# GpSimd's small work moved to other steps of attention, the router's last parts joined, and 28 constant matmuls ahead of the first expert's rows

## The chip, the core and the metric

One core of one Trainium2 chip runs the whole program. The metric is the time of one execution on the device in microseconds (us), lower is better. TensorE (PE) has two clock levels, 1.2 and 2.4 GHz; the profile prints the granted share, 0.50 or 1.00, or a mean of both over a stretch. VectorE is DVE, ScalarE is ACT, GpSimd is POOL; SyncE (SP) only issues DMAs, and POOL issues some too.

## What is computed

Clustered attention, then a mixture of 8 experts with one expert for each token, then a gated feed-forward block. Cut to what matters:

```python
# attention: 2 batches, 8 heads, 768 rows, 64 wide, 16 clusters
mask = q_assign[:, :, :, None] == k_assign[:, :, None, :]
scores = where(mask, scale * q @ k.T, -1e9)
attn_out = softmax(scores) @ v                 # 1536 rows of 512
# experts: 1536 rows, 8 experts, 512 -> 1024 -> 512
e_idx = argmax(x @ w_gate); gate_w = softmax(x @ w_gate)[e_idx]
out[rows of e] = gate_w * sigmoid(x @ w_output_gate)[e] * (relu(x @ w1[e]) @ w2[e])
# dense block: 512 -> 2048 -> 512
h = x @ w_in;  result = (h * sigmoid(h)) @ w_out
```

## The kernel before

**Attention.** The 16 heads go in 8 pairs of heads; a pair has 12 steps, so there are 96. A step is 128 query rows of one head. Its scores are made on PE (`qk_mm`, L371 and L373; the cluster mask is a second small product of KB and QB, the tiles that hold the mask rows `mk`), the row minimum on DVE (L392), the exponential on ACT (L394), which gives p in f32. Then p is split into a high and a low f16 part and turned, in one of two ways:

- by DMA: the high part by a copy on ACT (L403) or on DVE (L437, CAST, in steps 4, 5 and 8 of a pair), the low part by a subtraction on POOL (L438), and for two steps together one transposing DMA on SP's queue (L442), called T below;
- on PE, where `onpe` (L376) says so: PE transposes (L418, `turn`), high part on ACT (L424, `high`), low part on DVE (L429, `low2`, two instructions a step).

Seven steps later the product with v follows (`pv`, L462 to L464). A group of steps ends with a division on DVE (L469 to L471) that writes `xb`, the rows of attention's result.

Between the steps stands background work for the pairs that come next. `plan` (L256) gives each part a number r, the step of the pair at which it is issued: loads of q and k, their split (`halves`, ACT L330 and POOL L331, tiles nq and nk), their transposes and the copies of them to QA and KA (L178, L179), the DMAs that copy rows of QA to QB on POOL's queue and of KA to KB on SP's (L298), cluster scores and their one-hot (L193, L203 to L211), masks (L338 to L342), the scale of v (L123 to L142) and the split of v (`split_v`, POOL L152 to L156, for the two heads of a pair). `plan` is called with z true for the first pair. SP also writes zeros into the row buffers of the experts (`xst<-z`, L1195), one write behind most T DMAs. In attention every engine keeps the order in which the program issues; `run` (L476) is the loop over steps that sets this order.

**Router.** When a group of rows of `xb` is done, its part of the router runs as a generator whose pieces are issued one or two to a step: PE transposes (`xtp`, L680), a copy on ACT (L682), logits (`lg`, L689), their sum on DVE (`lacc`, L696), then `route` (L702): one-hot, ranks (`rk`, L731 and L734), gate value and slot on DVE (L723 to L761). Then POOL scatters the rows to the experts' buffers (`scatter`, L772, indirect DMAs, one for 128 rows). `overflow` (L787) counts the rows of each expert (`pn`, L791).

**Experts.** `moe1` (L983) loads and splits eight weight pieces ahead, then `prep(units[0])` reads the first expert's rows back (`xt<-xst`, L782) and turns them on PE (`etp`, L905); `expert` follows with `hp` (L948) and `yp` (L965). After the experts comes the dense block (L1146, L1158). The weights are split into two parts on ACT (L847) and on DVE or POOL (L852).

Of the kernel before, what the change touches and what calls it, by code (L numbers as in the profile page):

```python
# [11 lines left out]
F32 = mybir.dt.float32  # L12
# [18 lines left out]
class Att:  # L31
# [224 lines left out]
    def plan(s, pi, pairs, g0=None, vg=None):  # L256

        nc = s.nc
        u = []
        add = lambda r, f: u.append((r, f))  # L260
        nx = lambda g: lambda: next(g, None)
        if pi + 2 < len(pairs):
            add(3 if g0 else -1, lambda: s.load_qk(*pairs[pi + 2]))
        z = bool(g0)
        b, hp = pairs[pi]
        sp = lambda h, b=b, hp=hp: lambda: s.split_v(b, 2 * hp + h)
        if z:
            for r in (-1, 0, 0, 1, 1):
                add(r, nx(g0))
            for r in (3, 4, 4, 5, 6, 7, 8, 8):  # L270
                add(r, nx(vg))
        for h, r in enumerate((9, 10) if z else (-1, 0)):
            add(r, sp(h))
        if pi == 1:
            s.v1 = s.load_v(1)
        for r in {1: (3, 6, 10), 2: (6, 10), 3: (4, 5, 6, 6)}.get(pi, ()):
            add(r, nx(s.v1))
        if pi + 1 < len(pairs):
            b, hp = pairs[pi + 1]
            if z:  # L280
                for r in range(2):
                    add(r, lambda r=r: s.halves(pairs[1], r))
            hd = [None, None]
            ch = [None, None]
            oh = []

            def start(j):
                hd[j] = s.heads(2 * hp + j, j)
                if j == 0:
                    oh.append(s.ohp.tile([128, NT, 2, 2, C], BF16, tag='oh', name='oh'))  # L290

            def tr(j, a, half):
                if a == 0 and half == 0:
                    start(j)
                s.turned(hd[j][1 + 2 * a], s.nqk[b, hp][a], j, half, (-0.125, 1.0)[a])
                if half:
                    src, dst, e = ((hd[j][1][0:64], hd[j][2][0:64], nc.gpsimd), (hd[j][3][64:128], hd[j][4][0:64], nc.sync))[a]
                    s.defer.append(lambda: e.dma_start(dst.bitcast(F32), src.bitcast(F32)))  # L298

            def sc(j):  # L300
                s.scores(hd[j])
                ch[j] = s.best(s.clb, oh[0], j)
            bst = lambda j: lambda: next(ch[j])
            tr8 = [(j, a, half) for j in range(2) for a in range(2) for half in range(2)]
            for (j, a, half), r in zip(tr8, (2, 2, 3, 3, 4, 4, 5, 5) if z else (-1, -1, -1, 0, 0, 0, 3, 3)):
                add(r, lambda j=j, a=a, half=half: tr(j, a, half))
            for j, (r, r1, r2, r3) in enumerate(((4, 5, 6, 7), (6, 7, 8, 9)) if z else ((1, 2, 3, 4), (4, 5, 6, 7))):
                add(r, lambda j=j: sc(j))
                for q in (r1, r2, r3):
                    add(q, bst(j))  # L310

            def m():
                s.masks(oh[0], hd)
                for j in range(2):
                    s.ready[b, hp, j] = hd[j]
            add(9 if z else 8, m)
        if pi + 2 < len(pairs):
            for i, r in enumerate((5, 6) if not z else (9, 10)):
                add(r, lambda i=i: s.halves(pairs[pi + 2], i))
        u.sort(key=lambda x: x[0])  # L320
        return u
# [54 lines left out]
    def onpe(s, st):  # L376
        g = st['i'] // 2
        n = len(s.steps) // 2

        return (g % 3 == 0 and g >= 6) or g >= n - 6  # L380

    def dve(s, st):

# [65 lines left out]
    def pv(s, st):  # L449
        nc = s.nc  # L450
        b = st['b']
        h = st['hd'][0]
        t = st['t']
        pt = st['pt']
        g = st['g']
        gl = slice(g[0], g[-1] + 1)
        if t == g[0]:
            s.o = s.T('o2')[:, :NT * (D + 2)].rearrange('p (t d) -> p t d', t=NT) if st['j'] and st['pi'] == 7 and (g[-1] == NT - 1) else s.ps_o.tile([128, NT, D + 2], F32, tag='o', name='o')
        o = s.o
        vh, vl = s.vh[b, h]  # L460
        for kt in range(NT):
            nc.tensor.matmul(o[:, t, 0:D + 2], lhsT=pt[:, 0, kt], rhs=vh[:, kt], start=kt == 0, stop=False)  # L462
            nc.tensor.matmul(o[:, t, 0:D], lhsT=pt[:, 0, kt], rhs=vl[:, kt], start=False, stop=False)  # L463
            nc.tensor.matmul(o[:, t, 0:D + 2], lhsT=pt[:, 1, kt], rhs=vh[:, kt], start=False, stop=kt == NT - 1)  # L464
        if t == g[-1]:
            def ev():
                n = len(g)
                rs = s.sm.tile([128, NT], F32, tag='rs', name='rs')[:, :n]
                nc.vector.tensor_scalar(rs, o[:, gl, D], 1e-09, s.inv[b][:, 0, h:h + 1], op0=ALU.add, op1=ALU.mult)  # L469
                nc.vector.reciprocal(rs, rs)  # L470
                nc.vector.tensor_tensor(s.xb[b][:, gl, h * D:(h + 1) * D], o[:, gl, 0:D], rs.unsqueeze(2).to_broadcast([128, n, D]), op=ALU.mult)  # L471
                if h % 2 and s.router:
                    s.late.append((s.now + 1, b, h // 2, g))
            s.oev = ev

    def run(s):  # L476
# [4 lines left out]
        nc = s.nc  # L481
# [19 lines left out]
        traced = nc.cur_bb.bb.instructions  # L501
# [11 lines left out]
        rg = []  # L513
        free = False
        n = len(steps)
# [4 lines left out]
        while done < n:  # L520
# [15 lines left out]
            if 0 <= i < n:  # L536
                s.soft(steps[i])
            s.out()
            if 2 <= i < n + 2 and s.onpe(steps[i - 2]):
                s.low2(steps[i - 2])  # L540
            if 1 <= i < n + 1:
                (s.turn if s.onpe(steps[i - 1]) else s.low)(steps[i - 1])
            now = []
            while todo and todo[0][0] <= i - base:
                now.append(todo.pop(0)[1])
            for f in now[:len(now) // 2]:
                f()
            for k in range(3 if i >= n - 12 else 2):
# [5 lines left out]
                f()  # L554
            if s.late and i >= s.late[0][0]:
                rg.append(s.router(s, *s.late.pop(0)[1:]))
            for k in range(2):
                if rg and (k == 0 or (i - base) % 12 == 9 and i < n - 12) and (free or not (1 <= i < n - 12 and s.onpe(steps[i - 1]))):
                    x = next(rg[0], 0)
                    free = x == 'free'  # L560
                    if x == 0:
                        rg.pop(0)
# [3 lines left out]
        while rg or s.late:  # L566
            if not rg:
                rg.append(s.router(s, *s.late.pop(0)[1:]))
            for _ in rg.pop(0):
                pass  # L570

        prev = {}
        for ins in traced[first:]:
            if ins.engine in prev:
# [21 lines left out]
class Moe:  # L596
# [386 lines left out]
    def moe1(s, w2, free):  # L983
# [19 lines left out]
        def prep(u):  # L1003
            e, h, n = u
            xt = s.rows('xt', s.xo, slice(0, 128), 1) if e == E else s.rows('xt', s.xst, slice(e * CAP + h * 128, e * CAP + (h + n) * 128), n)
            X[u] = (s.labels(xt, n), s.lift(xt, n))
# [1 line left out]
        for i in range(N0):  # L1008
            item(order[0], i)
        s.hold = False  # L1010
        prep(units[0])
        with tc.issue_after(s.lastrow):
            for i in range(N0, 8):
                item(order[0], i)
# [209 lines left out]
```

## Time and profile before

| | |
|---|---|
| time, median of 3 (lowest to highest) | 864.39 us (862.42 to 864.69) |
| the profiled execution: time, span | 858.08 us, 856.0 us |
| mean granted clock of TensorE | 0.925 |
| PE, DVE, ACT, POOL busy in the span | 749.6, 501.9, 415.2, 328.6 us |

The profile is of one execution. Its times are in us from the span's start. A line number is that of the source above; an idle time in brackets stands before an instruction, with what ended it. Attention takes the first 321 us of the span, and the experts and the dense block the rest.

### The profile page before, as it was taken

Reading aid. Unit: us, or ns where it says so; the run is one execution under the profiler, and the core shown is the slowest. Engines: PE = TensorE matmul, PEld = TensorE weight load, DVE = VectorE, ACT = ScalarE, POOL = GpSimd, SP = SyncE. Lnnn points to the kernel's source line nnn. Section 1 sums busy time; section 2 is a strip of 40 time slices with the busy share of each in tenths; the row PEclk is TensorE's granted clock in tenths of the full one; section 3 lists DMA queues with packets and bytes.
Section 4 is the critical chain, followed back from the end, with each engine's and each line's share of the span. In section 5 each row is a group of like instructions: output and inputs, shape, how many; then the busy total and the mean of one; then the engine's idle time right before and its main releaser. Section 6 shows DMA issues by size and latency. Waiting matters only on the chain.

```text
span 856.0 us, 14041 instructions
## 1 busy us (share of the span) xinstructions
PE 749.6 (88%) x5416; PEld 636.4 (74%) x5416; DVE 501.9 (59%) x905; ACT 415.2 (48%) x659; POOL 328.6 (38%) x271
## 2 busy tenths in 40 slices
PE   5859897869799873999899999889899999999994
PEld 4649787868788863888797887567688788878883
DVE  6757688567867777475555687699932322232221
ACT  3756777557485654565444654465522322222221
POOL 1678758385685316644333454335400000000000
PEclk9658999789799985999999999979999999999997
DMA  4399999696676536688664864465400100010001
GB/s 150 65 221 243 205 183 155 134 184 126 136 169 129 121 112 231 217 305 267 210 212 156 295 215 152 172 227 172 148 1 1 49 1 1 0 50 1 1 0 52
DMA packets 135752, 117.09 MB, mean 137 GB/s; under 512 B 100823, under 2 KB 106967, under 8 KB 135680
## 3 DMA queue, kind: packets, MB, share of 16 engines
q1 hardware_dynamic: 131728, 107.06, 48.0%
q0 software_dynamic: 3952, 9.08, 3.7%
q8 instruction: 44, 0.72, 0.4%
q14 instruction: 28, 0.23, 0.1%
HBM read 71.67 MB, written 18.45 MB: 105 GB/s over the span
## 4 chain that ended last, share of the span: by engine, by line
PE 33%; DMA 5%; issue 5%; DVE 4%; POOL 2%; ACT 1%; ACTq 0%; POOLq 0%; DVEq 0%
PE op L1146 13%; PE hp L1158 13%; PE yp L965 3%; DMA x<-ys,f 3%; PE hp L948 2%; POOL w L852 2%; PE hr L930 2%; DMA stage<-in_moe_w_out 1%; DVE stage L1091 1%; DVE stage L1092 1%; DVE stage L1090 1%; DMA stage<-in_moe_w_in 1%; DMA stage<-in_moe_w 1%; DMA out_x<-os 0%; ACT w L847 0%
## 5 line engine op out<-in xcount | busy, mean ns | idle before, releaser
L852 POOL TENSOR_TENSOR w<-stage,w 128x512 fp32r<-128x512 f32 (+1 forms) x54 | 102.2, 1898 | 117.6 <-ACT w L847 115.8
L1158 PE MATMUL hp<-XH,w 128*128 128x512 f32 x384 | 128.5, 406 | 6.8 <-DVE sg L1166 5.6
L847 ACT ACTIVATE w<-stage 128x1024 fp32r<-128x1024 f32 (+1 forms) x104 | 96.4, 940 | 62.4 <-DVE stage L1092 29.9
L438 POOL TENSOR_TENSOR p<-p,p 128x768 f16<-128x768 f32 x60 | 98.4, 1650 | 72.7 <-DVE p L437 42.3
L392 DVE TENSOR_REDUCE m<-sp 128x1 f32<-128x768 f32 x96 | 91.0, 952 | 44.4 <-PE sp L373 35.3
L394 ACT ACTIVATE p<-sp,m 128x768 f32<-128x768 f32 x96 | 86.6, 902 | 54.1 <-DVE m L392 49.3
L1146 PE MATMUL op<-w,GH 128*128 128x512 f32 x384 | 111.7, 397 | 0.0
L1166 DVE TENSOR_TENSOR sg<-hp,sg 128x512 f32<-128x512 f32 x48 | 33.1, 689 | 118.2 <-ACT sg L1165 118.2
L948 PEld LDWEIGHTS hp<-X,w 128*128 128x128 f32 x672 | 86.8, 190 | 11.4 <-DVE HL L951 7.7
L948 PE MATMUL hp<-X,w 128*128 128x256 f32 x672 | 90.0, 284 | 4.6 <-DVE HL L951 4.2
L1158 PEld LDWEIGHTS hp<-XH,w 128*128 128x128 f32 x384 | 73.9, 193 | 26.1 <-DVE sg L1166 7.2
L852 DVE TENSOR_TENSOR w<-stage,w 128x1024 fp32r<-128x1024 f32 x50 | 70.8, 1426 | 28.5 <-ACT w L847 25.1
L462 PE MATMUL o<-vh,pt 128*128 128x66 f16 x576 | 67.7, 202 | 22.2 <-DMA pt<-p 15.9
L1165 ACT ACTIVATE sg<-hp 128x512 f32<-128x512 f32 x48 | 28.6, 597 | 119.5 <-PE hp L1158 118.5
L1146 PEld LDWEIGHTS op<-w,GH 128*128 128x128 f32 x384 | 73.3, 191 | 17.5
L1158 PE MATMUL hp<-XL,w 128*128 128x512 f32 x192 | 77.6, 404 | 2.6 <-DVE XL L852 2.6
L462 PEld LDWEIGHTS <-pt 128*128 128x128 f16 x576 | 55.9, 102 | 29.8 <-DMA pt<-p 17.5
L371 PE MATMUL sp<-KA,QA 128*128 128x384 f32 x192 | 65.8, 426 | 11.8 <-ACT p L394 11.4
L463 PE MATMUL o<-vl,pt 128*128 128x64 f16 x576 | 67.1, 198 | 0.8 <-POOL vl L156 0.8
L1146 PE MATMUL op<-w,GL 128*128 128x512 f32 x192 | 67.0, 399 | 0.6 <-DVE GL L852 0.5
L464 PE MATMUL o<-vh,pt 128*128 128x66 f16 x576 | 66.9, 199 | 0.0
L965 PE MATMUL yp<-w,HH 128*128 128x512 f32 x224 | 63.7, 399 | 0.3 <-ACT HH L950 0.3
(206 smaller groups left out, 1447.2 us busy)
## 6 DMA issues: line engine op xcount, KB each, us to landing
stage<-in_moe_w SPq DMA_DIRECT2D x72, 512.0 KB, 4.7
stage<-in_moe_w_in SPq DMA_DIRECT2D x16, 512.0 KB, 4.7
stage<-in_moe_w_out SPq DMA_DIRECT2D x16, 512.0 KB, 3.5
xst<-z SPq DMA_DIRECT2D x16, 258.0 KB, 3.2
xt<-xst SPq DMA_DIRECT2D x7, 516.0 KB, 4.0
vt<-in_v SPq DMA_DIRECT2D x4, 768.0 KB, 7.2
xt<-x SPq DMA_DIRECT2D x6, 512.0 KB, 5.2
out_x<-os SPq DMA_DIRECT2D x12, 256.0 KB, 2.4
```

Of the source, the lines that this page charges most:

```text
L392: st['min'] = nc.vector.tensor_reduce(m, sv, axis=AX.XY, op=ALU.min).ins
L394: st['exp'] = nc.scalar.activation(p32, sv, AF.Exp, bias=m, scale=-1.0).ins
L438: s.nc.gpsimd.tensor_sub(p16[:, 1], p32, p16[:, 0])
L462: nc.tensor.matmul(o[:, t, 0:D + 2], lhsT=pt[:, 0, kt], rhs=vh[:, kt], start=kt == 0, stop=False)
L463: nc.tensor.matmul(o[:, t, 0:D], lhsT=pt[:, 0, kt], rhs=vl[:, kt], start=False, stop=False)
L464: nc.tensor.matmul(o[:, t, 0:D + 2], lhsT=pt[:, 1, kt], rhs=vh[:, kt], start=False, stop=kt == NT - 1)
L847: s.nc.scalar.activation(hi, src, AF.Copy)
L852: (eng or s.nc.vector).tensor_sub(lo, src, hi)
L948: nc.tensor.matmul(hp, lhsT=W1[k][w][:, f * 128:(f + 1) * 128], rhs=x[:, k, :N], start=n == 0, stop=n == 11)
L965: nc.tensor.matmul(yp, lhsT=h[:, f, i * 128:(i + 1) * 128], rhs=w, start=n == 0, stop=n == 23)
L1146: nc.tensor.matmul(op[i], lhsT=g[:, i * 128:(i + 1) * 128], rhs=w, start=f == 0 and m == 0, stop=f == 15 and m == 2)
L1158: nc.tensor.matmul(hp, lhsT=I[k, f // 8][w][:, fs], rhs=x[:, k], start=n == 0, stop=n == 11)
```

## The change

It has four parts.

1. In `plan`, for the first pair the scale of v, the split of v, the one-hot of the second head and the split of q and k get other step numbers; for the other pairs the split of v moves from steps -1 and 0 to steps 1 and 2, and the split of q and k from steps 5 and 6 to steps 7 and 8.
2. `onpe` also takes the fourth pair of steps of the first pair of heads (steps 6 and 7), so these two are turned on PE, and one T DMA with its two POOL subtractions goes. In `run`, where a step turned on PE is followed by one turned by DMA, its two `low2` instructions stand behind the other step's own instructions, in the background list.
3. In the last two steps a finished group's router part is taken up at once and not a step later, and up to six pieces of it are issued to a step, each behind a `flush` of what was put off.
4. After attention's last PE instruction 28 matmuls of constants (128x128 by 128x512, bf16) are issued, and `prep(units[0])` behind them. Their result is used nowhere.

```diff
             for r in (-1, 0, 0, 1, 1):
                 add(r, nx(g0))
-            for r in (3, 4, 4, 5, 6, 7, 8, 8):
+            for r in (3, 3, 4, 4, 5, 6, 6, 6):
                 add(r, nx(vg))
-        for h, r in enumerate((9, 10) if z else (-1, 0)):
+        for h, r in enumerate((7, 9) if z else (1, 2)):
             add(r, sp(h))
...
-            for j, (r, r1, r2, r3) in enumerate(((4, 5, 6, 7), (6, 7, 8, 9)) if z else ((1, 2, 3, 4), (4, 5, 6, 7))):
+            for j, (r, r1, r2, r3) in enumerate(((4, 5, 6, 7), (7, 8, 8, 9)) if z else ((1, 2, 3, 4), (4, 5, 6, 7))):
...
-            for i, r in enumerate((5, 6) if not z else (9, 10)):
+            for i, r in enumerate((7, 8) if not z else (8, 10)):
                 add(r, lambda i=i: s.halves(pairs[pi + 2], i))
...
-        return (g % 3 == 0 and g >= 6) or g >= n - 6
+        return (g % 3 == 0 and g > 0) or g >= n - 6
...
-                    s.late.append((s.now + 1, b, h // 2, g))
+                    s.late.append((s.now + (s.now < len(s.steps) - 2), b, h // 2, g))
...
-            if 2 <= i < n + 2 and s.onpe(steps[i - 2]):
+            late = 2 <= i < n + 2 and s.onpe(steps[i - 2])
+            if late and (i - 1 >= n or s.onpe(steps[i - 1])):
                 s.low2(steps[i - 2])
+                late = False
...
+            if late:
+                now.append(lambda st=steps[i - 2]: s.low2(st))
...
-            for k in range(2):
-                if rg and (k == 0 or (i - base) % 12 == 9 and i < n - 12) and (free or not (1 <= i < n - 12 and s.onpe(steps[i - 1]))):
+            for k in range(2 if i < n - 2 else 6):
+                if i >= n - 2:
+                    s.flush()
+                if rg and (i >= n - 2 or k == 0 or (i - base) % 12 == 9 and i < n - 12) and (free or not (1 <= i < n - 12 and s.onpe(steps[i - 1]))):
...
+        s.lastpe = [x for x in traced if x.engine == s.nc.tensor.engine][-1]
...
-        prep(units[0])
+
+        idle = s.ps_h.tile([128, 512], F32, tag='h', name='idle')
+        with tc.issue_after(s.att.lastpe):
+            for _ in range(28):
+                r = nc.tensor.matmul(idle, lhsT=s.ones, rhs=s.tri.unsqueeze(1).to_broadcast([128, 4, 128]), start=True, stop=True)
+        with tc.issue_after(r.ins):
+            prep(units[0])
```

**SP in the first pair of heads.** KB<-KA are copies of turned keys, pt<-p is a T DMA, xst<-z a write of zeros, and the four `mk` DMAs bring the mask rows of the second pair of heads. Before:

```order
19 L298 DMA KB<-KA 64x768
20 L442 DMA_TRANSPOSE pt<-p_463 128x24x128
21 L1195 DMA xst<-z 128x516
22 L442 DMA_TRANSPOSE pt<-p_533 128x24x128
23 L1195 DMA xst<-z 128x516
24 L342 DMA QB<-mk 16x768
25 L342 DMA KB<-mk 16x768
```

Now:

```order
19 L298 DMA KB<-KA 64x768
20 L442 DMA_TRANSPOSE pt<-p_464 128x24x128
21 L1208 DMA xst<-z 128x516
22 L342 DMA QB<-mk 16x768
23 L342 DMA KB<-mk 16x768
```

The second T DMA and the write of zeros behind it no longer stand ahead of the `mk` DMAs.

**POOL where the fourth pair of heads begins** (the last steps of the third). L438 is the low part of p (p_1848 before and p_1865 now is the tile of the T DMA that PE waits for in the profile), vh and vl are the split of v, QB<-QA the copies of turned queries. Before:

```order
85 L438 TENSOR_TENSOR p_1848<-p_1846,p_1848 128x768
86 L152 MEMSET vh 128x6x2
87 L154 TENSOR_SCALAR vt_339<-vt_339,vsc_597 128x384
88 L155 CAST vh<-vt_339 128x6x64
89 L156 TENSOR_TENSOR vl<-vt_339,vh 128x384
90 L298 DMA QB<-QA 64x768
91 L438 TENSOR_TENSOR p_1848<-p_1887,p_1848 128x768
92 L152 MEMSET vh 128x6x2
93 L154 TENSOR_SCALAR vt_339<-vt_339,vsc_597 128x384
94 L155 CAST vh<-vt_339 128x6x64
95 L156 TENSOR_TENSOR vl<-vt_339,vh 128x384
96 L298 DMA QB<-QA 64x768
```

Now:

```order
83 L438 TENSOR_TENSOR p_1865<-p_1863,p_1865 128x768
84 L298 DMA QB<-QA 64x768
85 L438 TENSOR_TENSOR p_1865<-p_1904,p_1865 128x768
86 L298 DMA QB<-QA 64x768
87 L152 MEMSET vh 128x6x2
88 L154 TENSOR_SCALAR vt_339<-vt_339,vsc_548 128x384
89 L155 CAST vh<-vt_339 128x6x64
90 L156 TENSOR_TENSOR vl<-vt_339,vh 128x384
```

Both copies of queries and both low parts of the tile now stand ahead of both splits. It is so at the start of every later pair of heads.

**DVE at the end of attention.** L754 to L761 (now L761 to L768) finish the route of the last group but one, L469 to L471 divide the last rows, L696 (now L703) begins the route of the last group. Before:

```order
393 L429 TENSOR_TENSOR pt<-ptp,pt 128x384 x2
394 L696 TENSOR_TENSOR lacc_108<-lacc_108,lg 128x64
...
400 L469 TENSOR_SCALAR rs<-o_4856,vsc_2252 128x2
401 L470 RECIPROCAL rs<-rs 128x2
402 L471 TENSOR_TENSOR xb_67<-o_4856,rs 128x2x64
...
407 L746 TENSOR_REDUCE rank<-r_e_4906 128x4
...
415 L761 RECIPROCAL xb_67<-r_g 128x4
416 L696 TENSOR_TENSOR lacc_108<-lacc_108,lg 128x32
```

Now:

```order
401 L753 TENSOR_REDUCE rank<-r_e_4849 128x4
402 L429 TENSOR_TENSOR pt<-ptp,pt 128x384 x2
...
410 L768 RECIPROCAL xb_67<-r_g 128x4
411 L469 TENSOR_SCALAR rs<-o,vsc_2283 128x2
412 L470 RECIPROCAL rs<-rs 128x2
413 L471 TENSOR_TENSOR xb_67<-o,rs 128x2x64
414 L429 TENSOR_TENSOR pt<-ptp,pt 128x384 x2
415 L469 TENSOR_SCALAR rs<-o_4936,vsc_2283 128x2
416 L470 RECIPROCAL rs<-rs 128x2
417 L471 TENSOR_TENSOR xb_67<-o_4936,rs 128x2x64
418 L703 TENSOR_TENSOR lacc_108<-lacc_108,lg 128x32
```

Before, the last `low2` and the last division (row 402) stood ahead of the end of the first of these routes. Now they stand behind it, and PE likewise makes the last group's three products with v behind that route's ranks.

## Rows read from the trace of the kernel before

**Rows 1.** Stretches: us, length; PE, PEld, DVE, ACT, POOL busy (instructions); granted clock, DMA share, GB/s.

```profile
40.00:50.00 10.00, 4.68 (x23) 3.74 (x23) 9.65 (x25) 4.27 (x5) 6.08 (x4) 0.75 1.07 233
...
130.00:169.00 39.00, 31.95 (x369) 29.39 (x369) 26.41 (x53) 24.02 (x39) 23.11 (x22) 0.82 0.89 155
...
147.40:161.00 13.60, 9.19 (x75) 8.47 (x76) 7.39 (x19) 4.42 (x6) 3.43 (x3) 0.50 1.05 205
...
314.60:333.80 19.20, 3.16 (x49) 2.42 (x45) 14.99 (x62) 6.92 (x11) 9.64 (x10) 0.50 0.35 123
333.80:338.50 4.70, 4.14 (x19) 3.74 (x20) 2.90 (x10) 2.25 (x3) 3.48 (x5) 0.50 1.01 357
```

**Rows 2.** Waits between 20 and 345 us: total, times, longest.

```profile
PE o L462 <- DMA pt<-p: 15.9, 3, 7.3
...
PE sp L373 <- DMA KB<-mk: 5.4, 2, 3.4
```

**Rows 3.** Timeline of PE, the two long waits for T: start, duration.

```profile
151.81 0.24 PE L462 MATMUL o<-vh,pt 128*128 128x66 f16 x1 [6.84 <-DMA pt<-p]
...
190.77 0.24 PE L462 MATMUL o<-vh,pt 128*128 128x66 f16 x1 [7.29 <-DMA pt<-p]
```

**Rows 4.** Timeline of SP's queue ahead of the first of them.

```profile
137.26 0.86 SPq L298 DMA_DIRECT2D KB<-KA  x1
138.23 6.83 SPq L442 DMA_TRANSPOSE pt<-p  x1
```

**Rows 5.** Line L442 over the span: issue in ns, then issue to landing.

```profile
L442 SPq DMA_TRANSPOSE pt<-p x30: 3592/4128/9387, 35.0 to 282.8; - x30
...
DMA to landing us min/median/max: 5.4/6.8/13.7
```

**Rows 6.** Timeline of POOL at the same place.

```profile
134.57 0.58 POOL L298 DMA_DIRECT2D QB<-QA  x1
135.18 1.66 POOL L438 TENSOR_TENSOR p<-p,p 128x768 f16<-128x768 f32 x1
...
139.59 0.58 POOL L298 DMA_DIRECT2D QB<-QA  x1
```

**Rows 7.** Timeline of ACT at the same place.

```profile
133.72 0.87 ACT L179 ACTIVATE QA<-tp 128x384 fp32r<-128x384 f32 x2
```

**Rows 8.** Timeline of SP's queue in the first pair of heads.

```profile
55.29 3.68 SPq L442 DMA_TRANSPOSE pt<-p  x1
59.02 0.57 SPq L1195 DMA_DIRECT2D xst<-z  x1
```

**Rows 9.** DVE's lines L437 and L429: duration in ns, least, median, most.

```profile
L437 DVE CAST p<-p x21: 548/551/2544, 36.9 to 272.7; 128x768 f16<-128x768 f32 x21
...
L429 DVE TENSOR_TENSOR pt<-ptp,pt x72: 544/548/559, 72.8 to 313.0; 128x384 f16<-128x384 f32 x72
```

**Rows 10.** Timeline of DVE, the end of attention.

```profile
315.92 0.29 DVE L471 TENSOR_TENSOR xb<-o,rs 128x128 f32<-128x128 f32 x1
...
318.22 0.18 DVE L761 RECIPROCAL xb<-r_g 128x4 f32<-128x4 f32 x1
...
321.96 0.17 DVE L761 RECIPROCAL xb<-r_g 128x2 f32<-128x2 f32 x1
```

**Rows 11.** Timeline of POOL, the scatters of the last rows.

```profile
318.69 1.09 POOL L772 DMA_INDIRECT xst<-xb,slot  x1 [2.81 <-DVE xb L761]
...
324.47 1.96 POOL L772 DMA_INDIRECT xst<-xb,slot  x1 [0.30 <-DVE w L852]
326.74 0.98 POOL L772 DMA_INDIRECT xst<-xb,slot  x1 [0.30 <-issue]
```

**Rows 12.** Timeline of PE, the first expert.

```profile
333.77 1.97 PE L905 MATMUL etp<-ident,xt 128*128 128x128 f32 x8 [13.01 <-DMA xt<-xst]
...
348.94 0.39 PE L965 MATMUL yp<-w,HL 128*128 128x512 f32 x1
349.17 0.39 PE L965 MATMUL yp<-w,HH 128*128 128x512 f32 x1
```

## The prediction

> **What bounds the kernel now.** I read the stretches first, then PE's waits, then the queues behind the two longest waits, then the end of attention. The change moves nothing behind the first expert's first transposes, so its effect must arise before them: in attention, and in the hand-over to that expert. In attention no engine is full over a pair of heads. The pair from 130 to 169 has PE busy 31.95 of 39.00 us and DMA at 0.89 [rows 1]. PE's waits for DMAs show where the rest goes: three waits for the transposed p, 15.9 us together with the longest 7.3, and two for mask rows, 5.4 us together [rows 2]. The two long ones, 6.84 and 7.29 us, stand at the same place of two consecutive pairs, 39 us apart [rows 3]. In the hand-over PE has nothing to do for 13.01 us, because it waits for the rows read back [rows 12], and the clock granted from 314.6 to 338.5 us is 0.50, the lower of its two levels, so the first 4.70 us of the expert's work are done at half speed [rows 1].
>
> **Part 1, splits of v behind the copies and low parts (POOL), and `low2` behind CAST (DVE).** The first long wait ended at 151.81. Its T was issued at 138.23, 13.6 us before [rows 3, 4], against a median of 6.8 from issue to landing [rows 5]. Its issue itself took 6.83 us, against a median of 4.13 [rows 4, 5]. So this T meets other traffic, and one part of that can be named: a QB<-QA copy issued at 139.59 by POOL [rows 6], after the T. In the new order it stands behind the tile's second low part and ahead of both splits. It needs ACT's copy of the turned queries, which ends at 133.72 + 0.87 = 134.59 [rows 7]. So it can be issued at about 134.6, some 5 us sooner, and be out of the T's way. That is an added wait only for POOL: behind it stand the splits, whose first reader comes steps later. The first copy, 134.57 before, moves ahead of a low part and waits for ACT likewise, about 0.6 us of issue. The T does not start earlier for this: SP's queue is busy up to 138.12 with its own DMAs [rows 4], and only the chain behind the T before it moves, by two `low2` of 0.55 us that no longer stand ahead of the CAST [rows 9], 1.1 us.
>
> What the landing becomes is not in this trace. Bounds: 13.6 (no change, gain 0) and the median 6.8. I take the middle, 10.2, because the pair's loads of q and k and the copy of keys, which stay, are in flight at the same time. Then 3.4 + 1.1 = 4.5 a wait; a part of it is lost, since other waits are then late next (steps follow each other through DVE's minimum), so I take 4.0. Two waits: -8.0, with bounds 0 and -14.1. After the first wait the granted clock is 0.50 for 13.60 us, with PE busy 9.19 in it [rows 1]; a shorter wait may spare a part of this. Half of 9.19 is 4.6 at most for one of them, but PE isn't what sets the pace there; I take -1.0 for both, bounds 0 and -4. The split of q and k, which moves by two steps, and the splits of v in the other pairs lie in POOL's idle time (23.11 busy of 39.00 us [rows 1]): nothing. If that cover is gone, the low part of the next p is late by one split of v, 139.59 - 135.18 - 1.66 = 2.75 us [rows 6], and the T of that p with it.
>
> **Part 2, the first pair of heads.** SP loses a T and a write of zeros, 55.29 to 59.59 us [rows 8], ahead of the mask DMAs of the next pair, so these are issued 4.3 us sooner. PE's two waits for them, 5.4 us [rows 2], would then be over before PE is there. Two steps are turned on PE instead: four more `low2` of 0.55 us, 2.2 us on DVE [rows 9], less nothing, since the high part in these steps was not DVE's. DVE is full there: 9.65 of 10.00 us between 40 and 50 us, where PE has 4.68 and ACT 4.27 [rows 1], so the transposes and copies added to those two are hidden, and DVE's are not. From the other side POOL loses two low parts of 1.66 us [rows 6]. What a DVE instruction can lose beside POOL is seen in CAST: median 0.551, most 2.544 us [rows 9]. Sum: -5.4 + 2.2 = -3.2; since PE will not be at the second wait sooner than DVE lets it, I take -2.0, bounds -5.4 and +2.2.
>
> **Part 3, the router's last parts.** Before, the last division ran at 315.92, the last route but one ended at 318.22 + 0.18 = 318.40, and the last at 321.96 + 0.17 = 322.13 [rows 10]. The first of these routes no longer has the last four `low2` (2.2 us) ahead of it, but part of them were waits of DVE anyway: I take 0.8 us sooner, 317.6. The last group's division now comes behind it: two divisions of some 0.7 us each, two `low2` of 0.55, PE's three products and the transposes between: about 3.2 us, xb at 320.8. From the start of that division to the end of the route were 322.13 - 315.92 = 6.2 us, less 0.3 for the overlap with the other route: 326.7, so +4.6. The scatters bind the two together. Four of the first route went from 318.69 to about 324.2 [rows 11], now from 317.9 to 323.4. The last two, which began at 324.47 and ended at 326.74 + 0.98 = 327.72 [rows 11], 3.25 us, now begin at 326.8 and end at 329.1 (two of 0.98 and a gap of 0.30) to 330.1. From the end of the last scatter to PE's first transposes were 333.77 - 327.72 = 6.05 us [rows 11, 12], unchanged. So the rows come 1.4 to 2.4 us later; I take +2.2, that is 336.0. Bounds: -0.8 (the last route as early as the first) and +4.6.
>
> One of those scatters shows 1.96 us and not 0.98, beside DVE's weight split L852 that it waited on [rows 11]. The Trainium skill (SBUF — State Buffer, SBUF: two separate sides) says that DVE and GpSimd share one port pair as an exclusive lock, and the loser waits for the whole instruction. The trace agrees with its 1.96 and 2.544 beside 0.98 and 0.551. By the rule alone two late scatters that meet DVE's weight splits cost another 1.0, and the tail would be +3.2; the bounds above hold this.
>
> **Part 4, 28 matmuls of 512 columns.** Two such matmuls started 0.23 us apart at the full clock [rows 12], so 28 take 6.5 us at that, 13.1 at half. They start where PE ends its attention work, 333.77 - 13.01 = 320.76 before [rows 12], 1.4 ahead of the last route's end; now 326.7 - 1.4 = 325.3. At half clock from first to last they end at 338.4, 2.4 after the rows (336.0). If the clock rises after as much dense work as between 333.77 and 338.5, 4.7 us [rows 1, 12], then 10 of them take these 4.7 and 18 take 4.2: end at 334.2, before the rows, and the expert starts at the full clock, which gives back half of the 4.73 us, -2.4. I take -1.8, since the clock may be partly lost in the gap of 1.8 us. Bounds: -2.4 and +2.4.
>
> The Trainium skill (TensorE: Matmul & The Clock Gate, What's actually happening) calls the low clock the default, released by activity and lost by idling. This trace's 0.50 from 314.6 to 338.5 agrees. By the rule the matmuls can warm PE, but what ends before the rows can cool again; then the term is 0 and the sum 1.8 worse.
>
> **Sum.** -2.0 - 8.0 - 1.0 + 2.2 - 1.8 = -10.6. On the profiled execution: 858.08 - 10.6 = 847.5. That execution was 6.3 us below the median of the timed runs (864.39). I put the difference on the median: 853.8, so 854.0.
>
> **The rivals.**
>
> *Waits vanish.* If the copies of queries were the cause of the long landings, both T land at the median: the waits lose all of 14.1, the half clock behind them 3: 864.4 - 2.0 - 14.1 - 3 + 0.4 = 845.7, about 845. For it: two waits at one place of the pair, and 13.6 against 6.8. Against it: DMA at 0.89 of 39 us, so the traffic itself must be carried [rows 1].
>
> *DMA sets the pace.* The T is slow because loads of q and k, keys and zeros go at the same time, all of which stay. Then the waits stay: 864.4 - 2.0 + 0.4 = 862.8, give or take 2.5. For it: 0.89 over the pair and 1.05 in the stretch behind the wait [rows 1]. Its issue of 6.83 us began 1.4 us before the copy at 139.59 [rows 4, 6], which speaks against it little.
>
> *Slower: the tail.* Place: between the last division and the first expert's transposes. The last group's route ends 4.6 later and the 28 matmuls run at half clock to their end, 338.4, so the rows wait for PE: 338.4 - 333.8 = +4.6, and there is no clock gained. It decides where attention gives back less than this: with the T waits staying and the first pair at 0 the time is 869.0. For it: PE was at 0.50 with 3.16 busy of 19.20 us [rows 1] just before. Against it: dense work did bring the clock up at 338.5.
>
> **How the numbers follow.** My forecast 0.43 (own range 849 to 859), the waits vanish 0.15, DMA sets the pace 0.22, the tail 0.20. A difference under 0.3%, 2.6 us, can't be told from none here: faster is below 861.8. The first two lie there, 0.58, and of the third 0.08: faster 0.66, same 0.14, slower 0.20. The range: 845 leaves half of the second case below, 0.07, and 868 some 0.12 of the last above.
>
> **What would show it.** Right: the two long waits for T at 4 us or less and T's landing of 9 to 11 there, with QB<-QA issued ahead of it; the wait for mask rows of 3.4 gone; the last L768 at about 326.7, the last scatter's end near 329.5, and a clock of 1.00 in the first `hp`. Wrong: a wait of 6 us or more at the same place, a full DVE that makes the first pair longer, or PE in the 28 matmuls when the rows are there.

## The result and the profile after

The changed kernel took 856.07 us (median of 20 runs, 848.32 lowest) against 865.44 us for the kernel before, measured beside it. The ratio is 0.9862, 95% interval 0.9835 to 0.9889, which on 864.4 us is 11.9 us less, with 9.6 to 14.3 as the interval. The ratio leaves out the runs that lie over 1.5% above the fastest of their kernel (five of the 20, one of them 1068.87 us at a mean granted clock of 0.646, and one of the 20 of the kernel before); the medians of all runs differ by 9.4 us.

The profiled execution of the changed kernel took 859.21 us, span 857.1, no less than that of before (858.08). So a sum over the two spans explains nothing here. Each stage has to be read for itself, and the last part of this section says what went wrong in that execution.

**The two long waits.** The waits of PE in the changed kernel, in the same stretch and columns as [rows 2]:

```profile
PE o L462 <- DMA pt<-p: 4.1, 3, 1.7
...
PE sp L373 <- DMA QB<-mk: 2.1, 1, 2.1
...
PE sp L373 <- DMA KB<-mk: 0.7, 1, 0.7
```

The timeline of PE at the two places of [rows 3]:

```profile
143.91 0.23 PE L462 MATMUL o<-vh,pt 128*128 128x66 f16 x1 [1.74 <-DMA pt<-p]
...
177.18 0.24 PE L462 MATMUL o<-vh,pt 128*128 128x66 f16 x1 [1.53 <-DMA pt<-p]
```

The 6.84 and 7.29 us have become 1.74 and 1.53. The timeline of POOL ahead of the first of them, which answers to [rows 6]:

```profile
129.29 0.58 POOL L298 DMA_DIRECT2D QB<-QA  x1 [0.94 <-ACT QA L179]
129.90 1.67 POOL L438 TENSOR_TENSOR p<-p,p 128x768 f16<-128x768 f32 x1
131.71 0.53 POOL L298 DMA_DIRECT2D QB<-QA  x1
```

And SP's queue, which answers to [rows 4]:

```profile
133.06 0.51 SPq L298 DMA_DIRECT2D KB<-KA  x1
133.68 8.09 SPq L442 DMA_TRANSPOSE pt<-p  x1
```

The second copy of queries is issued 2.0 us before the T now, where it was 1.4 us behind it. The first waits 0.94 us for ACT, with nothing urgent behind. The issue of this T took 8.09 us all the same, more than the 6.83 of before. From minimum to minimum, the fourth pair takes 33.6 us where it took 38.8, and the fourth and fifth together 66.5 where they took 77.7. The first pair takes 36.2 us where it took 39.7; but its first minimum stood 2.7 us later in this execution (26.65 against 23.96), so its end came only 0.8 us sooner. Stretches of the changed kernel (columns as in [rows 1]), the first and fourth pair of heads:

```profile
26.60:62.80 36.20, 27.61 (x162) 23.32 (x161) 27.24 (x48) 25.60 (x37) 26.29 (x22) 0.86 0.63 137
...
127.10:160.70 33.60, 31.67 (x366) 29.19 (x364) 26.89 (x53) 23.68 (x39) 23.24 (x21) 0.85 0.92 179
```

**The end of attention.** The timeline of DVE, which answers to [rows 10]:

```profile
302.72 0.18 DVE L768 RECIPROCAL xb<-r_g 128x4 f32<-128x4 f32 x1
...
306.83 0.22 DVE L469 TENSOR_SCALAR rs<-o,vsc 128x2 f32<-128x2 f32 x1 [2.03 <-remote]
...
307.29 0.29 DVE L471 TENSOR_TENSOR xb<-o,rs 128x128 f32<-128x128 f32 x1
...
313.33 0.17 DVE L768 RECIPROCAL xb<-r_g 128x2 f32<-128x2 f32 x1
```

The timeline of POOL's last scatters, which answers to [rows 11]:

```profile
313.77 1.77 POOL L779 DMA_INDIRECT xst<-xb,slot  x1 [5.64 <-DVE o_cnt L801]
315.85 0.98 POOL L779 DMA_INDIRECT xst<-xb,slot  x1 [0.30 <-issue]
```

Four scatters of the first route are done early, at 308.14, and then POOL waits 5.64 us for the last route. The last minimum of attention in the timeline of DVE, in the profile of before and then here:

```profile
305.91 0.96 DVE L392 TENSOR_REDUCE m<-sp 128x1 f32<-128x768 f32 x1 [0.55 <-PE sp L373]
...
291.86 0.96 DVE L392 TENSOR_REDUCE m<-sp 128x1 f32<-128x768 f32 x1 [0.55 <-PE sp L373]
```

Measured from it, the last division came 10.0 us later before and 15.4 now, and PE's first transposes 27.9 us before and 30.8 now. Of the 15.4, 2.03 us are a stop of DVE, marked "remote" above: the trace has no releaser for it on this core.

**The clock.** Stretches of the changed kernel from the constant matmuls on:

```profile
312.00:317.10 5.10, 5.10 (x19) 1.79 (x16) 3.55 (x12) 4.93 (x7) 3.02 (x3) 0.50 0.13 46
317.10:323.90 6.80, 4.69 (x25) 2.30 (x23) 6.38 (x18) 0.55 (x2) 0.61 (x3) 1.00 0.66 229
323.90:330.70 6.80, 6.21 (x27) 5.85 (x28) 5.72 (x16) 3.53 (x6) 5.28 (x5) 0.50 0.97 341
```

And PE's timeline there:

```profile
317.29 3.40 PE L1022 MATMUL idle<-tri,ones 128*128 128x512 bf16 x15
322.65 1.10 PE L912 MATMUL etp<-ident,xt 128*128 128x128 f32 x8 [1.96 <-DMA xt<-xst]
324.49 0.80 PE L955 MATMUL hp<-X,w 128*128 128x256 f32 x2 [0.74 <-ACT X L854]
```

The clock rose after 5.1 us of the matmuls, close to the forecast (4.7). The matmuls ended at 320.69; the rows came at 322.65. PE then did eight transposes at the full clock, and at 323.90 the clock fell for 6.8 us, which is nearly all of the first expert's first blocks. What was won was lost again 1.25 us after the first transposes began.

**What went wrong in that execution.** At the first expert the start was 12.6 us sooner (324.49 for the first `hp` against 337.07), at the first `yp` 9.8 us (331.21 against 341.02), and at the last `yp` nothing of it was left (551.42 against 550.71). PE in the profile of before:

```profile
337.07 3.76 PE L948 MATMUL hp<-X,w 128*128 128x256 f32 x24
...
341.02 1.17 PE L965 MATMUL yp<-w,HH 128*128 128x512 f32 x4
```

The timeline of PE and then of ACT in the changed kernel:

```profile
332.21 1.58 PE L955 MATMUL hp<-X,w 128*128 128x256 f32 x12
...
341.71 0.80 PE L972 MATMUL yp<-w,HH 128*128 128x512 f32 x1 [4.23 <-ACT HH L957]
```

```profile
331.49 0.60 ACT L854 ACTIVATE X<-etp 128x512 fp32r<-128x512 f32 x1
341.28 0.38 ACT L957 ACTIVATE HH<-hp 128x256 fp32r<-128x256 f32 x1 [9.19 <-remote]
```

ACT stood still for 9.19 us, again without a releaser in the trace. The block that it was to read had been computed by 333.8. PE waited 4.23 us for it, and from 341.0 to 347.8 the granted clock was at 0.50 once more.

### The profile page after: what moved, and what is told of

It reads as the page before. It is cut to its first block, busy times and chain, and to the rows that moved or that the text cites. A ratio compares the mean times of both kernels' runs of the same rounds, so it can differ in the third digit from the quotient of the medians.

```text
span 857.1 us, 14129 instructions
## 1 busy us (share of the span) xinstructions
PE 764.6 (89%) x5456; PEld 644.3 (75%) x5456; DVE 503.5 (59%) x909; ACT 414.2 (48%) x661; POOL 325.3 (38%) x269
## 4 chain that ended last, share of the span: by engine, by line
PE 33%; DMA 6%; issue 5%; DVE 3%; POOL 3%; ACT 1%; ACTq 0%; POOLq 0%; DVEq 0%
PE op L1159 13%; PE hp L1171 12%; PE yp L972 3%; POOL w L859 3%; PE hp L955 2%; DMA x<-ys,f 2%; PE hr L937 2%; DMA stage<-in_moe_w_in 2%; DMA stage<-in_moe_w_out 1%; DMA stage<-in_moe_w 1%; DVE stage L1104 1%; DVE stage L1105 1%; DVE stage L1103 1%; DMA out_x<-os 0%; ACT w L854 0%
## 5 line engine op out<-in xcount | busy, mean ns | idle before, releaser
L1171 PE MATMUL hp<-XH,w 128*128 128x512 f32 x384 | 126.7, 404 | 9.6 <-DVE sg L1179 8.4
L438 POOL TENSOR_TENSOR p<-p,p 128x768 f16<-128x768 f32 x58 | 95.3, 1650 | 29.4 <-DVE p L437 21.9
L955 PEld LDWEIGHTS hp<-X,w 128*128 128x128 f32 x672 | 89.1, 196 | 13.7 <-DVE HL L958 9.2
L955 PE MATMUL hp<-X,w 128*128 128x256 f32 x672 | 93.3, 290 | 6.8 <-DVE HL L958 5.9
L462 PE MATMUL o<-vh,pt 128*128 128x66 f16 x576 | 67.4, 202 | 11.5 <-DVE xb L471 7.4
```

The costliest lines, as they stand in the source:

```text
L438: s.nc.gpsimd.tensor_sub(p16[:, 1], p32, p16[:, 0])
L955: nc.tensor.matmul(hp, lhsT=W1[k][w][:, f * 128:(f + 1) * 128], rhs=x[:, k, :N], start=n == 0, stop=n == 11)
L1171: nc.tensor.matmul(hp, lhsT=I[k, f // 8][w][:, fs], rhs=x[:, k], start=n == 0, stop=n == 11)
```

## The experiments

All ran in three groups, each beside the kernel before. The ratios are to it. The changed kernel itself stands at 0.9862 (first measurement) and 0.9888 (below).

**The changed kernel again.** No edit.

> The changed kernel once more, for a second profile. Theory H (a hitch): in the first profile ACT stood still for 9.2 us behind the third hidden block of the first expert, with no releaser in the trace, and all of the 12.6 us that the first expert's start had won was gone by the end of the first three experts; this belongs to that execution alone. Then here the start is 11 to 13 us sooner, at least 8 of them are still there at the last matmul, and the time is 848 to 858. Theory W (weights): the first experts wait for their weights, whose loads did not start sooner, so the gain is given back in every execution: then under 3 us are left at the last matmul in this profile too.

852.0 us, ratio 0.9888 (0.9849 to 0.9928), profiled execution 848.67. The timeline of ACT at the same place:

```profile
331.14 0.60 ACT L854 ACTIVATE X<-etp 128x512 fp32r<-128x512 f32 x1
333.50 0.39 ACT L957 ACTIVATE HH<-hp 128x256 fp32r<-128x256 f32 x1 [1.76 <-PE hp L955]
```

The first `hp` is 12.9 us sooner than before and the last matmul 9.6 us. Theory H holds and W falls: the stop belongs to an execution. With the half clock behind it the stop cost 7.5 us: a block of `hp` that starts 10.1 us after the first `yp` here (340.99 and 330.86) starts 17.6 us after it in the first profile (348.81 and 331.21). A stop of ACT of 3.0 to 9.2 us without a releaser, at this line, stands in the first profile of the changed kernel and in five others below, and not in the rest. From the first `yp` to the last matmul it was 503.1 us in the profile before, 503.6 here and 513.8 in the first profile of the changed kernel. It is not the only thing that varies there: another profile below has 511.4 without it. What holds ACT isn't known.

**The splits of v back ahead of the copies.**

```diff
-enumerate((7, 9) if z else (1, 2))
+enumerate((7, 9) if z else (-1, 0))
```

> The changed kernel with the split of v for the later pairs at steps -1 and 0 again. Theory Q: the late copies of queries (QB<-QA behind the splits on POOL's queue) lengthened the two T landings of 13.5 us; then the two long waits of PE for T come back, 5 to 7 us each, and the time is 8 to 12 us above the changed kernel's. Rival L: the order of low2 behind the CAST and the earlier start of the chain did it; then the waits stay under 2.5 us and the time is within 3 us of the changed kernel's.

858.43 us, ratio 0.9940 (0.9908 to 0.9972). The waits of PE and the timeline at the second of two that came back (5.99 and 6.44 us):

```profile
PE o L462 <- DMA pt<-p: 14.7, 5, 6.4
```

```profile
154.20 0.24 PE L462 MATMUL o<-vh,pt 128*128 128x66 f16 x1 [6.44 <-DMA pt<-p]
```

Here the copy is issued 2.7 us behind the T, and that T took 15.1 us to land. The time is 0.5 to 0.8% above the changed kernel's, 4.5 to 6.7 us, where 8 to 12 were expected. The waits came back in the size that Theory Q gives, but one pair earlier, at the third and fourth pair of heads; at the fifth only 0.64 us is left.

**`low2` back ahead of the next step.**

```diff
-if late and (i - 1 >= n or s.onpe(steps[i - 1])):
+if late:
```

> The changed kernel with low2 always ahead of the next step's own instructions, as before the change. Theory Q: the T chain starts 1.1 us later in the pairs that begin with PE steps, the waits grow by 1 us at most each, the time is 1 to 3 us above the changed kernel's. Rival L: the long waits come back, 5 us or more each, and the time is 8 to 12 us above.

853.77 us, ratio 0.9901 (0.9863 to 0.9940): 1 to 3 us above the changed kernel, within the intervals. The profile, an execution of 857.31 us, has waits of 6.3, 4.9, 2.6 and 4.1 us at the second to fifth pair. The longest stands at the second pair, where neither the kernel before nor the two profiles of the changed one have any:

```profile
PE o L462 <- DMA pt<-p: 18.6, 5, 6.3
```

By the waits the rival L was nearer, by the time Theory Q. The profiled execution lies 3.5 us above the median of the six (851.01 to 860.07), so the time counts.

**The first pair of heads back.** Undone in `plan` and `onpe` for z, here the core:

```diff
-for r in (3, 3, 4, 4, 5, 6, 6, 6):
+for r in (3, 4, 4, 5, 6, 7, 8, 8):
...
-return (g % 3 == 0 and g > 0) or g >= n - 6
+return (g % 3 == 0 and g >= 6) or g >= n - 6
```

> The changed kernel with the first pair of heads as before (its step numbers, and its steps 6 and 7 turned by DMA); everything else as changed. Expected from the two traces: the first pair takes 3.5 us more (39.7 and not 36.2 us), PE's wait of 3.4 us for mask rows is back, and the time is 2 to 4 us above the changed kernel's. Rival (a gain at the first pair is only moved, since the next pairs wait for DMAs): the second pair gives it back, and the time is within 1 us.

860.52 us, ratio 0.9978 (0.9945 to 1.0011), 8 to 10 us above the changed kernel, where 2 to 4 were expected. The first pair took 39.4 us and the wait for mask rows was back:

```profile
PE sp L373 <- DMA KB<-mk: 4.9, 3, 3.5
```

More was lost than the first pair has: the second took 38.3 us against 34.2.

**The second group. Without the 28 matmuls:**

```diff
-with tc.issue_after(r.ins):
-    prep(units[0])
+prep(units[0])
```

> The changed kernel without its 28 constant matmuls. In both profiles of the changed kernel the clock rose 5 us into them, stayed at 1.00 until 323.9 and fell again for 6.8 us, under the first hidden blocks: from the first transposes to the first yp matmul it took 8.5 us, against 7.25 before. Theory C (the clock won is lost again at once): without them that stretch is 7.0 to 7.5 us with the clock at 0.50 for its first 5 us, and the time is the same or 1 to 2 us less. Rival G (they give back what the prediction put down, 1.8 us): the stretch grows to 10 us or more and the time by 1.5 to 2.5 us.

855.89 us, ratio 0.9888 (0.9849 to 0.9926), the same as the changed kernel when run again. The stretch from the first transposes to the first `yp`:

```profile
325.95:334.30 8.35, 7.64 (x41) 7.24 (x41) 6.93 (x19) 4.34 (x7) 6.39 (x5) 0.58 0.93 330
```

8.35 us, against 8.56 in the changed kernel (8.48 when run again). Theory C holds: the 28 matmuls bought nothing. That it would be 7.0 to 7.5 was wrong; without them it was 6.8 to 8.4 in five profiles, and with them 7.1 to 8.6 in seven. In all these seven the granted clock fell behind them, where 1.9 to 3.5 us lay between their end and the transposes.

**38 matmuls.**

```diff
-for _ in range(28):
+for _ in range(38):
```

> The changed kernel with 38 constant matmuls, so that they end at about 322.7 us, when the rows are there (the 28 ended at 320.7, 2 us ahead). Theory C: with no gap ahead of the transposes the clock stays at 1.00 through the first hidden blocks; the stretch from the first transposes to the first yp matmul is 5 to 6 us, 2.5 to 3.5 us shorter, and of it 1 to 3 us are left in the time. Rival W (weights): that stretch is set by the arrival and splitting of the first weights; then it stays over 7.5 us whatever the clock.

853.51 us, ratio 0.9860 (0.9811 to 0.9909). PE's timeline, then the stretch:

```profile
325.29 0.81 PE L1022 MATMUL idle<-tri,ones 128*128 128x512 bf16 x3
326.56 1.09 PE L912 MATMUL etp<-ident,xt 128*128 128x128 f32 x8 [0.46 <-DMA xt<-xst]
```

```profile
326.56:332.86 6.30, 5.30 (x40) 4.62 (x41) 5.46 (x14) 4.11 (x7) 4.66 (x4) 1.00 1.01 365
```

With a gap of 0.46 us and not 1.96 the clock stayed at 1.00, and the stretch was 2.2 us shorter. In the time that can't be told from nothing (0 to 2 us).

**The router's last parts back.**

```diff
-for k in range(2 if i < n - 2 else 6):
-    if i >= n - 2:
-        s.flush()
-    if rg and (i >= n - 2 or k == 0 or ...
+for k in range(2):
+    if rg and (k == 0 or ...
```

and a finished group is taken up a step later again.

> The changed kernel with the router's last parts as before (taken up a step later, at most two pieces a step, no flush). Theory T: joining them made the last group's route 5.4 us later against the last minimum of attention (min to last division 10.0 us before, 13.8 to 15.4 now) and the rows 0.8 to 2.9 us later; undone, the rows come 1 to 3 us sooner after the last minimum (27.9 us after it) and the time is 1 to 3 us less, or the same where the 28 matmuls, which then end some 4 us ahead of the rows, lose the clock too. Rival: the first route's scatters, which start 13.7 us and not 15.5 us after the last minimum of the first pair of traces, decide; then undoing it costs 1 us.

846.42 us, ratio 0.9786 (0.9740 to 0.9831), the fastest of all. POOL's scatters run in one go:

```profile
306.77 0.97 POOL L777 DMA_INDIRECT xst<-xb,slot  x1 [0.31 <-issue]
308.05 1.38 POOL L777 DMA_INDIRECT xst<-xb,slot  x1 [0.30 <-issue]
```

From the last minimum (288.77) to PE's first transposes it took 26.4 us. Over all profiles: 26.4 to 28.1 in six with the order of before, 28.6 to 32.3 in eight with the joined parts; the means are 27.3 and 30.2. Joining cost 2.9 us by them. From the last minimum to the last division it was 10.0 us in all six and 13.8 to 16.8 in the eight (in three of these with a "remote" stop of DVE of 2.0 to 2.7 us in it). The ratio gives 0.8 to 1.0% or some 7 to 9 us, and the rest of this isn't accounted for (in its profile the last pair of heads but one was also 1.0 to 6.1 us shorter than in five others that have the same order of instructions there).

**The split of v alone**, on the kernel before.

```diff
-enumerate((9, 10) if z else (-1, 0))
+enumerate((9, 10) if z else (1, 2))
```

> The kernel before with one edit, the split of v for the later pairs at steps 1 and 2. Theory Q (copies of queries behind the splits lengthen two T landings): the two waits of 6.8 and 7.3 us fall under 4 us and the time is 6 to 9 us below before. Theory Q+L (undoing either edit alone brought waits of over 6 us back, so both are needed): the waits stay at 5 us or more, and the gain is 0 to 4 us.

860.48 us, ratio 0.9953 (0.9920 to 0.9986), a gain of 4.1 us. The waits of 6.8 and 7.3 us became 3.2 and 4.6:

```profile
PE o L462 <- DMA pt<-p: 13.3, 5, 4.6
```

Between the two expectations; Q+L is nearer by the gain.

**The third group. The router's last parts back and 44 matmuls.**

```diff
-for _ in range(28):
+for _ in range(44):
```

> The router's last parts as before, the rest as changed, and 44 constant matmuls in place of 28. With 28 they began at 303.6, the clock rose at 308.9, they ended near 312.5, 2.8 us ahead of the rows, and the clock fell from 315.7 to 322.5; 44 should end at about 316, with the rows (315.2). Theory C: the clock stays at 1.00, the stretch from the first transposes to the first yp matmul shrinks from 8.3 to 5.5 to 6.5 us as with 38 in the changed order (6.3), and the time is 0 to 2 us below the run with 28 (0.979 of before), so 0.976 to 0.981. That time also tells whether the large gain of putting the router's last parts back is there again. Rival: that gain was chance, and the ratio is 0.986 to 0.990 as for the changed kernel.

849.41 us, ratio 0.9807 (0.9766 to 0.9848). The gain of putting the router's parts back is there again. In its profile the 44 ran from 316.07 to 327.2, mostly at the full clock, so they were too few again:

```profile
329.68 1.97 PE L910 MATMUL etp<-ident,xt 128*128 128x128 f32 x8 [2.47 <-DMA xt<-xst]
```

The clock fell at 329.4, and the stretch was 8.1 us.

**Steps 6 and 7 of the first pair turned by DMA**, other step numbers as changed.

```diff
-return (g % 3 == 0 and g > 0) or g >= n - 6
+return (g % 3 == 0 and g >= 6) or g >= n - 6
```

> The changed kernel with steps 6 and 7 of the first pair turned by DMA again, its other step numbers as changed. Undoing both cost about 9 us. Theory S (SP's queue: the T and the zeros ahead of the mask DMAs do it): most of the 9 us, 5 or more, come from this one edit, the wait of 3.4 us for mask rows is back, and the ratio is 0.994 to 0.998. Rival N (the step numbers: scale and split of v earlier): then this costs under 3 us and the ratio stays at 0.986 to 0.991.

856.39 us, ratio 0.9891 (0.9839 to 0.9944), 0 to 2.5 us above the changed kernel. The first pair took 39.1 us and the wait was back:

```profile
PE sp L373 <- DMA KB<-mk: 6.1, 3, 4.5
```

So the first pair's shorter time is due to the T that is gone, and little of it is left in the time. Theory S falls, N holds by the time. That the step numbers alone are worth the rest of `pair0_back`'s 9 us is inferred from two ratios whose intervals end at 0.9944 and begin at 0.9945.

**The first pair alone**, on the kernel before: step numbers and `onpe` for z as changed.

```diff
-for r in (3, 4, 4, 5, 6, 7, 8, 8):
+for r in (3, 3, 4, 4, 5, 6, 6, 6):
...
-return (g % 3 == 0 and g >= 6) or g >= n - 6
+return (g % 3 == 0 and g > 0) or g >= n - 6
```

> The kernel before with the first pair of heads changed alone (step numbers, and steps 6 and 7 turned on PE). Undone alone it cost 8 to 9 us of the change's 10. If it stands by itself, the time is 5 to 9 us below before, with the first pair 3 to 3.5 us shorter. If it needs the other parts (rival), the two waits of 7 us for T, or others, take it back, and the gain is 0 to 3 us.

868.69 us, ratio 1.0035 (0.9999 to 1.0070): no gain, rather a loss of 0 to 6 us. The first two pairs took 70.5 us and not 75.2, and the third gave it all back:

```profile
115.64 0.24 PE L462 MATMUL o<-vh,pt 128*128 128x66 f16 x1 [6.29 <-DMA pt<-p]
```

A wait for T stood there that the kernel before did not have, and the two long ones stayed (6.4 and 7.9). The rival holds.

**`low2` behind the next step alone**, on the kernel before.

```diff
-if 2 <= i < n + 2 and s.onpe(steps[i - 2]):
+late = 2 <= i < n + 2 and s.onpe(steps[i - 2])
+if late and (i - 1 >= n or s.onpe(steps[i - 1])):
     s.low2(steps[i - 2])
+    late = False
...
+if late:
+    now.append(lambda st=steps[i - 2]: s.low2(st))
```

> The kernel before with one edit: low2 of a step turned on PE stands behind the next step's own instructions where that one is turned by DMA. Theory Q+L (T's chain 1.1 us sooner, each edit takes a part of the long waits): one or both waits of 7 us fall by 1 to 3 us, the gain is 1 to 4 us. Rival: 0, within 1.5 us, since SP's queue ahead of T is full anyway.

855.5 us, ratio 0.9898 (0.9858 to 0.9937): 8.8 us by this edit alone, far above both expectations. The waits, and SP's queue at the fourth pair:

```profile
PE o L462 <- DMA pt<-p: 4.2, 3, 2.1
```

```profile
131.74 3.61 SPq L442 DMA_TRANSPOSE pt<-p  x1
...
139.25 5.75 SPq L442 DMA_TRANSPOSE pt<-p  x1
```

From that pair's first minimum (132.94) the two T came -1.2 and +6.3 us, against 0.0 and +8.0 before. And POOL there:

```profile
136.96 0.58 POOL L298 DMA_DIRECT2D QB<-QA  x1
...
141.97 0.58 POOL L298 DMA_DIRECT2D QB<-QA  x1
```

The copy still stands 2.7 us behind the T, further than the 1.4 of before, and yet PE waited only 2.09 us. So a late copy alone does not make the long landing.

## Why the prediction was right, and where it was not

**The time.** 854.0 was forecast and 856.07 measured, in the range 845 to 868; by the ratio the change is worth 11.9 us, by the medians 9.4, and the sum had 10.6. The single terms came out less well than their sum: the waits gave somewhat more than was put down, the first pair alone and the matmuls nothing, and the tail took more. That they add up so well is in part luck.

**The T waits (-8.0 and -1.0).** The term of the waits holds in size. The two waits lost 9.5 to 10.9 us in the two profiles (14.1 before, 3.3 and 4.6 after), within the bounds, and the T landed in 10.5 and 11.5 us in the second, where 10.2 was taken and 13.5 was before. The first copy's wait for ACT (0.94 us) was as forecast and cost nothing seen. What the clock gave back (-1.0) isn't separated; over the fourth and fifth pair the mean granted clock was 0.85 before, 0.90 and 0.92 in the two profiles.

**The reason given for it holds only in part.** The step that the copy of queries, ahead of both splits, is out of the T's way carried 3.4 of each 4.5, and the step that the chain moves by two `low2` (1.1 us) the rest. Measured alone, the `low2` edit gave 8.8 us and the splits 4.1; undone alone, they cost 1 to 3 and 4.5 to 6.7. So they act on the same waits and do not add; alone the `low2` edit, put at 1.1 us, was the stronger, and undone alone the splits were. The waits for T at the third to fifth pair add up to 14.1 and 20.6 us in the two profiles with both old orders (the kernel before and `pair0_only`), to 3.3 to 7.8 in the eight with both new ones, and to 4.2 to 13.1 in the four with one of each. That the two orders together take the waits is shown; how each does it is not.

The `low2` part was mis-sized at least in that an earlier T was credited with its own start alone: with it the zeros, the loads of q and k and the copy of keys behind it on SP's queue start sooner too, and the next T came 1.7 us earlier against the pair. But an early T is not enough either: in `pair0_only`, with both old orders, T was issued 6.6 us after the first minimum of the fourth pair, and PE still waited 6.41 us for it. What changed most is the landing, and its cause stays open. With the copy 2.7 us behind the T, at +6.3 us in the pair, PE got it 10.9 us after its issue in one profile (`low2` alone) and 15.1 us in another (splits back).

**The first pair (-2.0).** It lost 3.5 us in the profile, more than forecast, by the mechanism named: the wait for mask rows of 3.43 us fell to 2.15, and both such waits from 5.4 to 2.8, where the text let them vanish. In the time it is worth nothing alone (1.0035), because the third pair's T is then late; undone alone it costs 8 to 10 us. The step that failed is the tacit one that a pair's gain reaches the end; the wait that was late next was a T, and it is the other edits that take it away.

**The tail (+2.2).** Right in sign and about right in size: +2.9 by the means over the profiles, and the last division, with the last route behind it, 5.4 and 3.8 us late in the two profiles where the text has +4.6 for the route. The first route's scatters ended early for nothing, since the last two decide. What was cited of the exclusive port (the Trainium skill, SBUF — State Buffer, SBUF: two separate sides) agrees with one of the last two scatters, 1.77 us beside DVE's work and 0.98 for the next. This part of the change costs time; taking it out gave the fastest kernel, 0.9786, and more than the 2.9 us explain.

**The 28 matmuls (-1.8).** Wrong, the term is 0: without them the ratio is the same, 0.9888. They did warm the clock, in 5.1 us where the text has 4.7, and their end 2.0 us ahead of the rows is what it forecast (1.8). The step that failed is "the clock may be partly lost in the gap": it was wholly lost, from 323.9 to 330.7. The rule of the Trainium skill that was weighed there (TensorE: Matmul & The Clock Gate, What's actually happening; idle brings the low clock back) was the better guide: its sum was 1.8 us worse. With the gap at 0.46 us the clock stayed.

**The rivals.** Of the three "Waits vanish" was nearest for attention: of 14.1 us of waits some 10 went. "DMA sets the pace" falls, since the DMA share in the pair is 0.92 now and the waits are short. "The tail" named the right cost but not the size, and the matmuls were done before the rows.

**Not tested.** In the later pairs the split of q and k also moved by two steps. The text puts it at nothing, and no run has it alone.

## What to carry to other kernels

A transposing DMA that is waited for is best seen as the end of a chain through a DVE instruction, a POOL instruction and everything ahead of it on its queue; what stands at the head of the chain can be worth more than its own duration (an edit put at 1.1 us gave 8.8 alone). A gain in one stage is only worth what the next DMA wait leaves of it, so each edit of a schedule is to be measured alone and undone alone. Work that is to keep the clock up has to last until the real work is there: here the clock fell in all eight profiles with a gap of 1.9 to 3.5 us and stayed in the one with 0.46 us, and even that gain was too small to be told in the time. And one profile is one execution: stages with the same order of instructions differed by up to 6 us between profiles.

## What was not expected of the hardware

ACT stood still for 3.0 to 9.2 us at the same line of the first expert in six of fourteen profiles, with no releaser in the trace, and DVE for 1.6 to 2.7 us near the end of attention in eight. DVE's stop appears in versions with and without each edit. ACT's appears in six of the ten profiles in which the split of v stands at its new steps and in none of the four in which it does not, too few to say whether that is chance; the same program had it in one profile and not in the next. With the half clock behind it, it hid 7.5 us of a 10 us gain in a single execution. Whether executions that were not profiled have such stops, no run here shows.
